# Attention and MLP in one kernel: the same instructions in another planned order, from a new table of key shifts

## The chip, the cores and the metric

The kernel runs on one core of one Trainium2 chip. The metric is the time of one execution on the device, in microseconds. All executions do the same work on the same inputs.

## What is computed

Attention with random features, followed by a two-layer MLP, in float32 on both sides.

```python
batch, n_heads, seq, head_dim = (8, 8, 576, 64)     # q, k, v; omega is 128 x 64
def phi(x):                                         # x is q or k, scaled by 64 ** -0.25
    proj = np.einsum('bhsd,md->bhsm', x, omega)
    h = proj - np.sum(x * x, axis=-1, keepdims=True) / 2.0
    return np.exp(h - np.max(h, axis=-1, keepdims=True)) / np.sqrt(m)
kv = np.einsum('bhsm,bhsd->bhmd', k_p, v)
z = np.sum(k_p, axis=2)
num = np.einsum('bhsm,bhmd->bhsd', q_p, kv)
den = np.einsum('bhsm,bhm->bhs', q_p, z)[..., None] + 1e-06
attn_out = num / den
...
h = x @ w_in                                        # x: 4608 tokens x 512; w_in 512 x 2048
g = h * (1.0 / (1.0 + np.exp(-h)))
return g @ w_out                                    # w_out 2048 x 512
```

## The kernel before

**Attention.** The 64 pairs of batch and head are worked in 32 windows of two heads each. A window projects k and q by omega on TensorE (L372 and L377 for the first eight windows, which fold the squares into the matmul; L372 for the others, with the middle rows apart at L386, L387 or L392). VectorE (DVE) takes the row maxima (L403, L405, L408) and makes biases of them (L411, L412), ScalarE (ACT) takes the exponentials (L433; for a few windows DVE adds the bias at L450 and L443 first and ACT does the whole at L454), GpSimd (POOL) sums the features of k (L462 to L475), and TensorE forms the z sums (L484), the product of features and v (L492), and a transpose of that (L500) through copies on ACT (L497, L505). DVE works out the denominators (L516, L522), POOL divides (L527), TensorE transposes the result (L533), ACT copies it (L537), and TensorE makes the numerator (L554). ACT casts or copies that into xq (L576), and for the first three batches DVE makes the low part (L580).

**MLP.** Every float32 product is done as three float32r products of a high and a low part (L725). Weights come in as 64-bit words that DVE turns into float32 (L607 on ACT, L619, L621 and L625 on DVE) and that ACT and POOL split (L635, L639). Token block 0 is multiplied directly: first layer into the PSUM pool h, ACT's silu (L736, L737), DVE's low part (L741, the unit g_low), second layer into the pool acc. The other eight blocks go in four pairs by a seven-product Strassen scheme, whose operands ACT and DVE split (L767, L771, L783, L787), and whose sums DVE forms (L763, L779, L817, L844). The MLP has 3120 matmuls in all, 576 into ps_h (the first layer of blocks 0 to 2) and 2544 into ps_acc; attention's small matmuls are put between them.

**What sets the order.** The whole program is a list of 3731 units, each with an engine, an assumed duration, what it must come after, the ring buffers and PSUM banks that it takes and frees, and a key: the time at which it is due. Plan.run fills the five engines' lists: of the units that could start at about the soonest moment on an engine it takes the one with the smallest key. Each engine then runs its list strictly in order, and the semaphores make sure of the dependencies. Before planning, keys are shifted by a table, STIR. Each of its 33 entries has a seed, a size and a range of keys; a unit whose key (under 900) lies in the range has its key moved by size times a number from -1 to 1, a hash of the seed and the unit's name. So the table draws one of very many nearby orders; the units, their instructions and their dependencies are the same in each. PSUM has eight banks in three pools, acc 4, h 2 and att 2; before the MLP starts and between its stages attention may take banks of the others, whichever comes free first, so the name of the pool (ps_acc, ps_h, ps_att) can differ for the same unit.

The lines that set this:

```python
            key = u["key"]
            if key < 900.0:
                for seed, size, lo, hi in STIR:
                    if lo <= key < hi:
                        u["key"] += size * (zlib.crc32((str(seed) + repr(n)).encode()) / 2**31 - 1)
...
                p = min((p for p in pick if p[3] <= least + 0.25), key=lambda p: p[2:])
```

## Time and profile before

| what | value |
|---|---|
| median of three runs | 994.75 us (993.66 to 995.33) |
| the profiled execution | 993.29 us |
| its span, first to last instruction | 991.2 us |
| granted clock, mean | 0.998 |
| ACT's table loads between exp and silu | 72 |

The profile is of one execution. A row of a group has the busy time, the mean of one instruction in ns, and the idle time of the engine just before such instructions with what ended it. PE is TensorE, PEld its weight loads, which run beside the matmuls. A busy PE is not always PE at its peak: the ends of matmuls are modelled. A releaser is inferred from semaphores, and where several were waited for the last by the profile is named.

The two parts of the work differ: until about 72 us only attention and the preparation of the weights run; from there to about 800 us attention's remaining windows are woven into the MLP; the rest is the MLP alone.

### The profile page before, as it was taken

The page shows a single profiled execution, that of the slowest core. Times are in us where ns is not written, and L with a number is a line of the kernel's source. Part 1 is how long each engine was busy: PE and PEld are TensorE (multiplying, and loading weights), DVE is VectorE, ACT ScalarE, POOL GpSimd, SP SyncE. Part 2 cuts the span into 40 slices and gives each one's busy share as a digit, 9 for nine tenths or more (in the row PEclk, how much of TensorE's full clock was granted, in tenths as well). Part 3 has the DMA queues.
Part 4 walks back from the last instruction along what each step waited for, and adds up shares of the span by engine and source line. Part 5 has one row for each costly group of instructions (what it writes and reads, how often), then busy time and mean ns, then how long its engine had stood idle before and what let it go on. Part 6 is the DMA issues. An engine that isn't in the chain of part 4 may idle for free.

```text
span 991.2 us, 17002 instructions
## 1 busy us (share of the span) xinstructions
PE 962.2 (97%) x5846; PEld 772.7 (78%) x5846; DVE 779.0 (79%) x1611; ACT 645.7 (65%) x1239; POOL 410.5 (41%) x427
## 2 busy tenths in 40 slices
PE   8889999999999999999999999999999999999998
PEld 7667777777778777777887777788788887888886
DVE  3999999589554898986988999797699966269954
ACT  7899776679778776859758856555275544325442
POOL 3775665867975666686331334333012210000000
PEclk9999999999999999999999999999999999999999
DMA  7579897899988788988667666666555566556562
GB/s 282 160 264 312 311 298 241 309 331 316 293 304 295 252 290 275 302 292 287 215 209 238 212 197 220 229 222 203 184 187 176 179 205 235 192 190 213 193 215 103
DMA packets 103734, 238.70 MB, mean 241 GB/s; under 512 B 13664, under 2 KB 44512, under 8 KB 103648
## 3 DMA queue, kind: packets, MB, share of 16 engines
q1 hardware_dynamic: 103504, 237.54, 71.7%
q8 instruction: 47, 0.77, 0.3%
q14 instruction: 39, 0.32, 0.1%
q10 hardware_dynamic: 144, 0.07, 0.0%
HBM read 193.53 MB, written 44.04 MB: 240 GB/s over the span
## 4 chain that ended last, share of the span: by engine, by line
PE 68%; DVE 16%; ACT 10%; issue 2%; DMA 2%; SPq 0%; DVEq 0%; ACTq 0%
PE ps_acc L725 50%; PE ps_h L725 6%; DVE prod L516 3%; PE ps_att L372 2%; DVE ts L771 2%; PE ps_att L492 2%; DVE g L621 2%; PE ps_h L372 2%; DVE g L619 1%; ACT hk L433 1%; PE ps_att L554 1%; DVE g L625 1%; ACT hq L433 1%; PE ps_att L533 1%; DVE g L763 1%
## 5 line engine op out<-in xcount | busy, mean ns | idle before, releaser
L725 PE MATMUL ps_acc<-ts,w 128*128 128x512 f32 x2544 | 612.3, 394 | 2.0 <-DVE ts L771 1.4
L725 PEld LDWEIGHTS ps_acc<-ts,w 128*128 128x128 f32 x2544 | 468.8, 188 | 102.4 <-DVE ts L771 2.5
L767 ACT CAST ts<-g 128x1024 fp32r<-128x1024 f32 x112 | 118.5, 1062 | 96.5 <-PE ps_acc L725 92.3
L771 DVE TENSOR_TENSOR ts<-g,ts 128x1024 fp32r<-128x1024 f32 x112 | 147.4, 1324 | 37.5 <-ACT ts L767 36.8
L527 POOL TENSOR_TENSOR hq<-hq,rd 128x384 f32<-128x384 f32 x84 | 90.6, 1104 | 168.9 <-DVE rd L522 151.6
L725 PE MATMUL ps_h<-xq,w 128*128 128x512 f32 x576 | 149.6, 400 | 2.5 <-ACT g L758 1.8
L725 PEld LDWEIGHTS ps_h<-xq,w 128*128 128x128 f32 x576 | 104.3, 188 | 25.3 <-ACT g L758 2.6
L817 DVE TENSOR_TENSOR g<-ps_acc,g 128x512 f32<-128x512 f32 x144 | 95.3, 685 | 32.3 <-PE ps_acc L725 31.1
L763 DVE TENSOR_TENSOR g<-g,g 128x1024 f32<-128x1024 f32 x64 | 84.4, 1340 | 5.8 <-ACT g L758 5.5
L462 POOL TENSOR_TENSOR t<-hk 128x256 f32<-128x256 f32 x64 | 53.5, 851 | 74.3 <-ACT hk L454 46.6
L516 DVE CUSTOM_DVE_ANT_0 prod<-hq,ps_att 128x128 f32<-128x128 f32 (+1 forms) x170 | 48.6, 286 | 19.2 <-PE ps_att L484 9.5
L475 POOL TENSOR_TENSOR es<-t,es 128x256 fp32r<-128x256 f32 x32 | 28.4, 889 | 68.2 <-ACT es L471 68.1
L639 POOL TENSOR_TENSOR w<-g,w 128x512 fp32r<-128x512 f32 x32 | 46.6, 1471 | 21.1 <-ACT w L635 18.2
L821 ACT ACTIVATE g<-g 128x1024 f32<-128x1024 f32 x36 | 37.5, 1058 | 26.5 <-DVE g L817 26.3
L783 ACT CAST ts<-xq 128x1024 fp32r<-128x1024 f32 x21 | 22.2, 1059 | 45.6 <-PE ps_acc L725 45.4
L467 POOL TENSOR_TENSOR t<-t,hk 64x128 f32<-64x128 f32 x64 | 40.2, 628 | 11.2 <-ACT hk L433 7.2
L353 ACT ACTIVATE nat<-nat 128x576 f32<-128x576 f32 x48 | 32.3, 705 | 14.5 <-DMA nat<-kn 7.9
L787 DVE TENSOR_TENSOR ts<-xq,ts 128x1024 fp32r<-128x1024 f32 x21 | 27.8, 1324 | 16.8 <-ACT ts L783 16.8
L433 ACT ACTIVATE hk<-ps_att,nbk 128x128 f32<-128x128 f32 x115 | 32.8, 404 | 7.0 <-DVE nbm L411 3.9
L433 ACT ACT_TABLE_LOAD x24 | 30.8, 1283 | 9.8 <-DVE nbk L412 7.4
L844 DVE TENSOR_TENSOR c<-ps_acc,c 128x512 f32<-128x512 f32 x48 | 30.7, 682 | 5.6 <-PE ps_acc L725 5.6
L358 DVE TENSOR_REDUCE sq<-nat 128x9 f32<-128x576 f32 x48 | 34.7, 745 | 0.4
(209 smaller groups left out, 1537.1 us busy)
## 6 DMA issues: line engine op xcount, KB each, us to landing
w<-w_d SPq DMA_DIRECT2D x168, 512.0 KB, 4.2
w<-ws_d SPq DMA_DIRECT2D x48, 512.0 KB, 3.3
rawk<-kT SPq DMA_DIRECT2D x32, 352.0 KB, 4.3
rawq<-qT SPq DMA_DIRECT2D x32, 352.0 KB, 3.9
v<-v SPq DMA_DIRECT2D x32, 320.0 KB, 4.5
out<-c SPq DMA_DIRECT2D x17, 512.0 KB, 4.5
g<-w_in SPq DMA_DIRECT2D x16, 512.0 KB, 5.3
g<-w_out SPq DMA_DIRECT2D x16, 512.0 KB, 4.4
```

The costliest lines, as they stand in the source:

```text
L372: nc.tensor.matmul(ps[:, cols], raw[r, o : o + P], w[r], start=True, stop=n not in FOLD)
L433: nc.scalar.activation(h[:, c], ps[:, i * M : (i + 1) * M], AF.Exp, bias=bias_of(n, who, c), scale=-1.0 if n in FOLD else 1.0)
L462: nc.gpsimd.tensor_tensor(t[:, i], e[:, 5 * i : 5 * i + 2], e[:, 5 * i + 2 : 5 * i + 4], ALU.add)
L467: nc.gpsimd.tensor_tensor(t[r, i - 3, 0], t[r, i - 3, 0], e[r, MID], ALU.add)
L516: nc.vector.tensor_tensor_reduce(out=prod[r], in0=e[r, c], in1=z[r, j * M : (j + 1) * M], scale=1.0, scalar=GUARD, op0=ALU.mult, op1=ALU.a ...
L527: nc.gpsimd.tensor_tensor(e[:, c], e[:, c], rd[:, c].unsqueeze(2).broadcast_to([P, 3, M]), ALU.mult)
L639: nc.gpsimd.tensor_tensor(lo, T["w", i], hi.bitcast(F32), ALU.subtract)
L725: nc.tensor.matmul(ps, w(a), x[:, b], start=first and n == 0, stop=last and n == 2, **more)
L763: nc.vector.tensor_tensor(out, a, b, ALU.subtract)
L767: nc.scalar.copy(g[:, 0], T["g", p, SOURCE[j], u])
L771: nc.vector.tensor_tensor(g[:, 1], T["g", p, SOURCE[j], u], g[:, 0].bitcast(F32), ALU.subtract)
L817: nc.vector.tensor_tensor(to, T["q", p, chain, i], T["g", p, r, i // 2][:, i % 2], ALU.add)
```

## The change

STIR has a new table of 107 entries, each with a fifth number, a mask. A unit's key is moved by an entry only where the hash has none of the mask's bits: with mask 0 all units of the range are moved, with 1 half of them, with 31 one in 32. 31 entries have mask 0, 12 have 1, 17 have 3, 16 have 7, 12 have 15 and 19 have 31. Sizes go from 0.18 to 10.75 (before, from 0.75 to 4.0). Two entries have empty ranges. The old entry that moved every unit under 900 by up to 0.75 is gone; the four entries over the whole span have masks 31, 7, 31 and 15.

```diff
 STIR = (
-    (85063, 0.75, -100, 900), (45882, 1.5, 786, 906), (7545, 0.75, 621, 741), (21412, 1.5, 610, 640),
...
+    (80956, 2.1, -110, 900, 31), (60897, 0.19, -80, 910, 7), (37960, 0.73, -90, 900, 31),
...
 )
...
         for n, u in self.units.items():
             key = u["key"]
-            if key < 900.0:
-                for seed, size, lo, hi in STIR:
-                    if lo <= key < hi:
-                        u["key"] += size * (zlib.crc32((str(seed) + repr(n)).encode()) / 2**31 - 1)
+            for seed, size, lo, hi, mask in STIR:
+                if key < 900.0 and lo <= key < hi:
+                    h = zlib.crc32((str(seed) + repr(n)).encode())
+                    if not h & mask:
+                        u["key"] += size * (h / 2**31 - 1)
```

Every line of the file behind the table stands 20 lower: L725 of before is L745 now, L533 is L553, L580 is L600, and so on. Over the whole list TensorE has 170 stretches of attention between MLP matmuls, where it had 165, and ACT has 74 table loads where it had 72.

**TensorE, end of the lead-in.** Where the MLP's first matmuls (ps_h<-xq,w) stand among the last attention units of windows 3 to 5: transposes of window 3 (ps<-ident,hq), the transpose of window 4's product (ident,kt), the projection of window 5's q (omn,rawq; half,c), the numerator of window 3 (en,kw), window 4's sums (es,ones). Before:

```order
L533 MATMUL ps_att<-ident,hq 128x128 x6
L533 MATMUL ps_h<-ident,hq 128x128 x3
L500 MATMUL ps_acc<-ident,kt 128x128
L372 MATMUL ps_att<-omn,rawq 128x128 x2
L377 MATMUL ps_att<-half,c 128x128 x2
...
L554 MATMUL ps_acc<-en,kw 64x512 x2
L554 MATMUL ps_acc<-en,kw 64x64 x2
L484 MATMUL ps_acc<-es,ones 128x256 x2
L386 MATMUL ps_acc<-omn,rawq 128x128
L387 MATMUL ps_acc<-half,c 128x128
L725 MATMUL ps_h<-xq,w 128x512 x24
```

The same place now:

```order
L553 MATMUL ps_att<-ident,hq 128x128 x6
L553 MATMUL ps_h<-ident,hq 128x128 x3
L406 MATMUL ps_acc<-omn,rawk 128x128
L407 MATMUL ps_acc<-half,c 128x128
L745 MATMUL ps_h<-xq,w 128x512 x3
L574 MATMUL ps_att<-en,kw 64x512 x2
L574 MATMUL ps_att<-en,kw 64x64 x2
L745 MATMUL ps_h<-xq,w 128x512 x6
L520 MATMUL ps_acc<-ident,kt 128x128
L504 MATMUL ps_acc<-es,ones 128x256 x2
L745 MATMUL ps_h<-xq,w 128x512 x15
L392 MATMUL ps_att<-omn,rawq 128x128 x2
```

The first 24 MLP matmuls have moved ahead of window 5's projection of q, nine of them ahead of window 4's transpose, three ahead of window 3's numerator.

**DVE, the same place.** Maxima (L405), a weight's words (L619, L621, L625), sums of squares of windows 8 and 9 (L358), denominators of window 4 (prod,den), the low part of xq of window 3 (the last L580), and the first g_low (ts<-ph). Before:

```order
L580 TENSOR_TENSOR xq<-ps_acc,xq 128x512
L358 TENSOR_REDUCE sq<-nat 128x9 x2
L625 SCALAR_TENSOR_TENSOR g_742<-g_632,g_742 128x512
L405 TENSOR_REDUCE nbq<-ps_att 128x4 x2
...
L516 ISA prod,den<-hq,ps_acc 128x128
L516 ISA den 128x1
L580 TENSOR_TENSOR xq<-ps_acc,xq 128x512
...
L522 RECIPROCAL rd<-den 128x9
L403 TENSOR_REDUCE nbq<-ps_acc 128x1
L619 TENSOR_SCALAR g_742<-g_687 128x512
...
L741 TENSOR_TENSOR ts<-ps_h,ts 128x512
```

The same place now, from the last L580 (L600) on:

```order
L600 TENSOR_TENSOR xq<-ps_att,xq 128x512
L536 ISA prod,den<-hq,ps_acc 128x128
...
L542 RECIPROCAL rd<-den 128x9
L761 TENSOR_TENSOR ts<-ps_h,ts 128x512
L641 SCALAR_TENSOR_TENSOR g_970<-g_970 128x512
L645 SCALAR_TENSOR_TENSOR g_970<-g_852,g_970 128x512
L761 TENSOR_TENSOR ts<-ps_h,ts 128x512
L425 TENSOR_REDUCE nbq<-ps_att 128x4 x2
L423 TENSOR_REDUCE nbq<-ps_acc 128x1
L378 TENSOR_REDUCE sq<-nat 128x9 x2
```

The low part of xq stands ahead of all of window 4's denominators, and the first two g_low stand ahead of window 5's maxima and of the sums of squares.

**TensorE, the middle projection of window 8.** The k projection of window 8 (oms,rawk x8), the matmul of its middle rows (the single oms,rawk and oms,rawq), and window 7's transposes. Before:

```order
L372 MATMUL ps_att<-oms,rawk 128x128 x8
L725 MATMUL ps_h<-xq,w 128x512 x9
L725 MATMUL ps_acc<-ts,w 128x512 x6
L392 MATMUL ps_att<-oms,rawk 128x128
L392 MATMUL ps_att<-oms,rawq 128x128
L533 MATMUL ps_att<-ident,hq 128x128 x3
```

Now:

```order
L392 MATMUL ps_att<-oms,rawk 128x128 x8
L745 MATMUL ps_h<-xq,w 128x512 x3
L745 MATMUL ps_acc<-ts,w 128x512 x9
L745 MATMUL ps_h<-xq,w 128x512 x3
L553 MATMUL ps_att<-ident,hq 128x128 x6
L745 MATMUL ps_h<-xq,w 128x512 x3
L412 MATMUL ps_att<-oms,rawk 128x128
L412 MATMUL ps_att<-oms,rawq 128x128
L553 MATMUL ps_att<-ident,hq 128x128 x3
```

Three more MLP matmuls and the first six of window 7's nine transposes stand ahead of the middle projection.

**DVE, the same place.** From the end of window 7's denominators (rd<-den) to the subtraction that empties window 8's two banks (hk<-ps_att,nbk). Before:

```order
L522 RECIPROCAL rd<-den 128x9
L741 TENSOR_TENSOR ts<-ps_h,ts 128x512
L619 TENSOR_SCALAR g_1964<-g_1872 128x512
L619 TENSOR_SCALAR g_1974<-g_1877 128x512
L621 SCALAR_TENSOR_TENSOR g_1974<-g_1974 128x512
L625 SCALAR_TENSOR_TENSOR g_1974<-g_1877,g_1974 128x512
L621 SCALAR_TENSOR_TENSOR g_1964<-g_1963,g_1964 128x512
L405 TENSOR_REDUCE mxk<-ps_att 128x4 x2
L411 TENSOR_TENSOR nbk<-mxk,sq 128x2x4
L412 SCALAR_TENSOR_TENSOR nbk<-nbk,sq 128x2x4
L450 TENSOR_TENSOR hk<-ps_att,nbk 128x512 x2
```

Now:

```order
L542 RECIPROCAL rd<-den 128x9
L761 TENSOR_TENSOR ts<-ps_h,ts 128x512
L641 SCALAR_TENSOR_TENSOR g_1970<-g_1970 128x512
L645 SCALAR_TENSOR_TENSOR g_1970<-g_1898,g_1970 128x512
L425 TENSOR_REDUCE mxk<-ps_att 128x4 x2
L431 TENSOR_TENSOR nbk<-mxk,sq 128x2x4
L432 SCALAR_TENSOR_TENSOR nbk<-nbk,sq 128x2x4
L470 TENSOR_TENSOR hk<-ps_att,nbk 128x512 x2
```

Two L619 and an L621 that stood between the g_low and the maxima now stand ahead of the denominators.

35 rows, old and new, of the table STIR are left out of this document.

## The prediction

> **What bounds the kernel now.** I read the page first, for the shares and the clock, then the stretches, then TensorE's waits, and last the timeline at the two longest waits. The first lines of the page give the shares over the whole span.
>
> ```profile
> span 991.2 us, 17002 instructions
> PE 962.2 (97%) x5846; PEld 772.7 (78%) x5846; DVE 779.0 (79%) x1611; ACT 645.7 (65%) x1239; POOL 410.5 (41%) x427
> ```
>
> TensorE is busy for 962.2 of 991.2 us, so 29.0 us are idle, and an order that changes no work can win at most those, and part of what is slow inside the busy time. The stretches, cut where the character of the work changes, say where the 29 us lie. The columns are the length, then the busy time of PE, PEld, DVE, ACT and POOL with instruction counts, the granted clock, and DMA.
>
> ```profile
> 25.00:72.00 47.00, 37.54 (x394) 29.40 (x391) 44.19 (x125) 42.43 (x128) 35.77 (x39) 0.96 0.64 209
> 72.00:125.00 53.00, 50.40 (x310) 40.22 (x310) 48.98 (x95) 46.63 (x87) 32.75 (x30) 1.00 0.92 312
> 125.00:250.00 125.00, 120.75 (x790) 95.49 (x787) 102.93 (x266) 97.45 (x174) 85.48 (x90) 1.00 0.89 297
> 250.00:500.00 250.00, 245.17 (x1540) 194.47 (x1539) 185.31 (x424) 184.67 (x404) 166.19 (x166) 1.00 0.83 280
> 500.00:965.00 465.00, 464.56 (x2492) 376.04 (x2490) 376.74 (x663) 250.40 (x395) 82.64 (x87) 1.00 0.63 205
> ```
>
> Idle PE time is 9.46 us from 25 to 72, 2.60 from 72 to 125, 4.25 from 125 to 250, 4.83 from 250 to 500, and 0.44 in the 465 us after that. The second half is bound by TensorE and has nothing left for an order to win. The lead-in is another matter: from 25 to 72 us DVE is busy for 44.19 of 47 us, so it is DVE that bounds it, and only 2.81 us of DVE idle can be squeezed there. What TensorE waited for, longest in total first (columns: us, times, longest):
>
> ```profile
> PE ps_att L372 <- ACT en L537: 2.4, 2, 1.7
> PE ps_att L392 <- DVE hk L450: 1.9, 1, 1.9
> PE ps_h L725 <- ACT g L758: 1.8, 3, 0.8
> PE ps_att L533 <- POOL hq L527: 1.5, 2, 1.1
> PE ps_acc L533 <- POOL hq L527: 1.5, 4, 0.6
> PE ps_acc L725 <- DVE ts L771: 1.4, 3, 0.6
> PE ps_acc L500 <- DMA rawk<-kT: 1.3, 1, 1.3
> PE ps_h L725 <- DVE ts L741: 0.7, 1, 0.7
> ```
>
> No kind of wait is large: the total is many single waits of about 1 us, each at a place of its own. A new order must therefore be judged place by place, and the two largest places are looked at here.
>
> **Term 1, the end of the lead-in.** In the timeline of TensorE at 61 to 71 us (start, length, line, tiles, and in brackets the idle time before it and its releaser):
>
> ```profile
> 61.32 0.55 PE L533 MATMUL ps_h<-ident,hq 128*128 128x128 f32 x3
> 63.13 0.33 PE L500 MATMUL ps_acc<-ident,kt 128*128 128x128 f32 x1 [1.26 <-DMA rawk<-kT]
> 65.13 0.76 PE L372 MATMUL ps_att<-omn,rawq 64*128 64x128 f32 x3 [1.68 <-ACT en L537]
> ...
> 70.92 5.73 PE L725 MATMUL ps_h<-xq,w 128*128 128x512 f32 x24
> ```
>
> Between 61.9 and 65.1 us TensorE does one transpose, and the MLP's first matmul comes at 70.92. The clock answers to that lull, in two stretches just behind it:
>
> ```profile
> 64.00:66.00 2.00, 0.87 (x10) 0.78 (x12) 2.00 (x3) 2.00 (x8) 1.15 (x1) 1.00 0.11 30
> 66.00:68.00 2.00, 2.00 (x25) 2.00 (x23) 2.00 (x4) 2.00 (x8) 0.74 (x2) 0.52 0.11 15
> 68.00:70.00 2.00, 2.00 (x10) 0.95 (x10) 1.73 (x3) 1.88 (x6) 2.00 (x2) 0.63 0.87 299
> ```
>
> The granted clock is 0.52 and 0.63 for 2 us each, which loses 2 x 0.48 + 2 x 0.37 = 1.70 us of TensorE. Together the place costs TensorE 1.26 + 1.68 + 1.70 = 4.64 us. [...]
>
> The new order (first pair of excerpts of the change) puts three of the first 24 L725 matmuls ahead of the numerator of window 3, six more before the L500 transpose that waited, and the other fifteen before the projection that waited; before, all 24 stood behind these. What they need is there earlier: DVE (second pair) writes xq for window 3 (L580) before the denominators of window 4, not in their midst, and the two L405 of window 5 and the two L358 now stand behind the first L741. By their rows those are
>
> ```profile
> 66.22 1.40 DVE L358 TENSOR_REDUCE sq<-nat 128x9 f32<-128x576 f32 x2
> 68.45 1.28 DVE L405 TENSOR_REDUCE nbq<-ps_att 128x4 f32<-128x512 f32 x2
> 71.63 0.69 DVE L580 TENSOR_TENSOR xq<-ps_acc,xq 128x512 fp32r<-128x512 f32 x1
> ```
>
> 1.40 + 1.28 = 2.68 us, taken from in front of the MLP's first g_low (L741) and put behind it; the L580 is 0.69. It is moved, not removed. Ahead of the numerator of window 5 the plan lists 137 units on DVE before and 139 now, the two more, on balance, being one L621 of a weight and one L741, by the means of their groups (the number behind the busy time, in ns)
>
> ```profile
> L621 DVE SCALAR_TENSOR_TENSOR g<-g 128x512 uint32<-128x512 uint32 x16 | 15.6, 975 | 2.4 <-ACT g L607 1.4
> L741 DVE TENSOR_TENSOR ts<-ps_h,ts 128x512 fp32r<-128x512 f32 x16 | 10.9, 682 | 3.4 <-ACT ps_h L737 3.1
> ```
>
> 0.975 + 0.682 = 1.7 us more. So the two bounds are a gain of 2.81 us (DVE's idle gone) and a loss of 1.7 us (DVE as idle as before, and more to do by then). I take a gain of 2.0, near the upper end, because TensorE's own lull and its slow clock lie exactly where matmuls are put.
>
> **Term 2, the middle projection of window 8.** The longest single wait of the span behind the first 10 us is here; TensorE first, then DVE:
>
> ```profile
> 162.26 1.16 PE L372 MATMUL ps_att<-oms,rawk 64*128 64x128 f32 x16
> 163.35 2.34 PE L725 MATMUL ps_h<-xq,w 128*128 128x512 f32 x9
> 165.53 1.52 PE L725 MATMUL ps_acc<-ts,w 128*128 128x512 f32 x6
> 168.92 0.46 PE L392 MATMUL ps_att<-oms,rawk 128*128 128x128 f32 x2 [1.87 <-DVE hk L450]
> 169.52 0.52 PE L533 MATMUL ps_att<-ident,hq 128*128 128x128 f32 x3
> ```
> ```profile
> 161.26 2.07 DVE L619 TENSOR_SCALAR g<-g 128x512 uint32<-128x512 uint32 x2
> 164.70 0.69 DVE L621 SCALAR_TENSOR_TENSOR g<-g,g 128x512 uint32<-128x512 uint32 x1
> 165.30 1.28 DVE L405 TENSOR_REDUCE mxk<-ps_att 128x4 f32<-128x512 f32 x2
> 168.08 1.29 DVE L450 TENSOR_TENSOR hk<-ps_att,nbk 128x512 f32<-128x512 f32 x2
> ```
>
> L392 needs a PSUM bank that L450 empties at about 168.8. Before, 15 L725 matmuls stand between the L372 that fills the banks and L392; now (third pair of excerpts) 18 stand there and six L533 as well. The three more cost 3 x 1.52 / 6 = 0.76 us, the six L533 about 2 x 0.52 = 1.04, together 1.80 us of useful work in the place of a wait of 1.87. On DVE (fourth pair) two L619, two L621 and an L625 stood between the L741 and this L405, 4.04 us from 161.26 to 165.30; now one L621 and one L625 do, so L405 no longer has to come 1.9 us after the L372 that ends at 163.4. Bounds: a gain of 1.87, or nothing if the denominators that now stand ahead of the L741 make DVE late by as much. I take 1.5.
>
> **Term 3, the other waits from 72 to 500 us.** They are 2.60 + 4.25 + 4.83 - 1.87 = 9.81 us, in many places, all of which the new order rearranges. I can't follow each, so I count in the plan's order the handoffs with the least room: transposes (L533) with fewer than six L725 matmuls between their last POOL step and themselves, 13 of windows 4 to 31 before and 10 now, and sums (L484) with as few behind L475, 9 before and 7 now. That is 5 of 22, or 23%, which of 9.81 us is 2.2. But the trace shows only six waits for L527, 3.0 us (rows above), of which none is a microsecond long but one, so what is tight in the list is mostly not late on the chip, and I take half: 1.0. Bounds: a gain of 4.9 (half of them gone), and a loss of 4.9 (half as many again).
>
> **What costs nothing.** The new order has 74 loads of an activation table instead of 72. A load, with its neighbours on ACT:
>
> ```profile
> 170.07 0.48 ACT L537 COPY en<-ps_att 128x384 f32<-128x384 f32 x1 [3.26 <-PE ps_att L533]
> 170.57 1.28 ACT L454 ACT_TABLE_LOAD   x1
> 171.87 1.17 ACT L454 ACTIVATE hk<-hk 128x1152 f32<-128x1152 f32 x1
> ```
>
> It takes 1.28 us and the neighbours stand within 0.02 us of it, so two more are 2.57 us of ACT, which is busy 65% of the span: cover enough, and without the cover 2.57 us on the path. [...] From 500 us on PE has 0.44 us to win, and the list of PE ends in one run of 672 L725 (738 before), and the last four stores stand as they stood: nothing there.
>
> **The sum.** 2.0 + 1.5 + 1.0 = 4.5 us. The profiled execution took 993.29 us (span 991.2 and 2.09 around it), so 988.8 for such an execution. The median of the three runs shown is 994.75, which is 1.46 above it, so the forecast for a median is 990.3 us.
>
> **The rivals.** A measurement of this kernel can tell 0.2%, about 2.0 us, from no change.
>
> *DVE gives nothing back (no change).* The lead-in is DVE's, and DVE's work ahead of window 5 is no less. Then terms 1 and 3 are nothing, and term 2's 1.5 us is all: 993.3. For it speaks 44.19 of 47 us; against it, that DVE is down to 48.98 of 53 and 102.93 of 125 us in the stretches behind, so something other than DVE holds TensorE there too.
>
> *The matmuls pulled forward block the queue (slower).* TensorE runs its list in order. The tenth to twelfth L725 need xq of window 3, which the L554 behind the third feeds through ACT's cast and L580; behind them stand the projections of window 5 (L372, L386), and DVE, ACT and POOL of window 5 behind those. If the L725 wait, window 5 and all after it comes late. The cast costs
>
> ```profile
> 63.97 0.61 ACT L576 CAST xq<-ps_acc 128x512 fp32r<-128x512 f32 x1
> ```
>
> Price: the 1.7 us more that DVE has ahead of window 5, the 2.81 us that DVE then idles once more, and a new wait of cast and L580 (0.61 + 0.69 = 1.30 us): 5.8 us, less term 2's 1.5: 4.3 us more, 999.1. It decides if the wait at those L725 is over about 3 us; below that DVE has other work queued to fill it. For it speaks that only six L725, a transpose and an L484 lie between that L554 and the ones that need it; against, that L580 stands early in DVE's new list.
>
> *Most single waits go (faster by far).* If the order fits the chip as a whole, term 1 gives DVE's 2.81 and the slow clock's 1.70, term 2 all of 1.87, term 3 half of 9.81: 11.3 us, 983.5. Against it: each place has to fit by itself.
>
> **How the numbers follow.** The forecast of a gain of 2 to 7 us has a chance of 0.46, the far gain 0.17, no change 0.15, the blocked queue and its like 0.22. So faster by over 0.2% is 0.63, within 0.2% 0.15, slower 0.22. The terms' own bounds make 994.75 - 2.81 - 1.87 - 4.9 = 985.2 and 994.75 + 1.7 + 4.9 = 1001.4 if all fall one way; the range reaches down to include the far gain and up past the blocked queue's 999.1: 982 to 999.5.
>
> **What would show it.** Right: no dip of the clock between 60 and 75 us, the first L725 (L745 in the new file) at about 68, PE idle from 25 to 72 down by 2 us or more, no wait over 1 us at L392's successor L412, and 500 to 965 unchanged. Wrong: PE idle before 250 us of 16 us again with the waits at other lines, a wait of 3 us or more at the first 24 L745, or idle PE behind 500 us, where there was none.

## The result, and the profile after

The changed kernel takes 1007.81 us (median of 4 runs, 1006.23 to 1010.3), the kernel before beside it on the same chip 994.2 us (992.87 to 995.33). The ratio is 1.0140, 95% interval 1.0115 to 1.0165: slower by 13.6 us, where 4.5 us less had been forecast, and beyond the upper end of the range. The profiled execution took 1010.3 us, its span is 1008.4 us, its mean granted clock 0.989 (0.998 before). One of the six executions of f3_three below, the profiled one, had a clock of 0.751 and took 1197.94 us; its row leaves that execution out, and its profile is not used.

The first lines of the page of the changed kernel:

```profile
span 1008.4 us, 17035 instructions
PE 970.0 (96%) x5846; PEld 777.1 (77%) x5846; DVE 785.4 (78%) x1611; ACT 650.1 (64%) x1241; POOL 408.4 (40%) x427
```

The same matmuls keep TensorE busy 7.8 us longer, and it is idle for 38.4 us instead of 29.0: 9.4 more. The busy part is the clock: 1.1% of 1008.4 us is 11 us at a stopped clock, 0.2% of 991.2 was 2, so 9 us more are lost to it. That holds for these two executions: over all on record the mean clock is 0.990 for the changed kernel and 0.996 for the kernel before, which makes 6 us. The stretches say where (columns as in the prediction):

```profile
25.00:72.00 47.00, 39.58 (x369) 30.72 (x370) 43.11 (x122) 42.68 (x123) 31.52 (x37) 0.93 0.69 228
72.00:125.00 53.00, 49.29 (x321) 39.44 (x321) 47.68 (x92) 43.14 (x90) 30.64 (x28) 1.00 0.86 293
125.00:250.00 125.00, 119.76 (x793) 94.22 (x790) 106.33 (x248) 94.39 (x169) 87.69 (x90) 1.00 0.89 298
250.00:500.00 250.00, 239.97 (x1483) 188.29 (x1482) 177.27 (x406) 186.32 (x398) 160.04 (x159) 0.99 0.82 270
500.00:965.00 465.00, 461.56 (x2487) 374.46 (x2486) 379.87 (x689) 252.63 (x405) 88.61 (x93) 0.99 0.62 203
```

Idle TensorE in them: 7.42, 3.71, 5.24, 10.03 and 3.44 us, before 9.46, 2.60, 4.25, 4.83 and 0.44. The first stretch has the 2 us that the first term promised. All others are worse, and the worst are the two behind 250 us. The waits that are new, or grew (us in total, times, longest):

```profile
PE ps_acc L745 <- DVE c L864: 6.9, 2, 3.8
PE ps_h L553 <- POOL hq L547: 3.2, 4, 1.7
PE ps_att L553 <- ACT hk L453: 3.1, 2, 1.8
PE ps_h L745 <- DVE xq L600: 2.2, 1, 2.2
PE ps_att L553 <- DVE hk L470: 2.1, 1, 2.1
```

The largest did not exist before: MLP matmuls that wait for L864 (L844 before), where DVE adds the last sums of a Strassen pair from the acc banks. TensorE at the first of the two places:

```profile
446.82 1.55 PE L745 MATMUL ps_acc<-ts,w 128*128 128x512 f32 x6
452.19 5.06 PE L745 MATMUL ps_acc<-ts,w 128*128 128x512 f32 x11 [3.82 <-DVE c L864]
```

DVE there (left out are window 20's maxima and biases, between the first two sums, and then the rest of window 18's denominators):

```profile
444.92 0.68 DVE L864 TENSOR_TENSOR c<-ps_acc,c 128x512 f32<-128x512 f32 x1
...
447.44 0.68 DVE L864 TENSOR_TENSOR c<-ps_acc,c 128x512 f32<-128x512 f32 x1
448.05 0.28 DVE L536 CUSTOM_DVE_ANT_0 prod<-hq,ps_h 128x128 f32<-128x128 f32 x1
...
451.38 0.21 DVE L542 RECIPROCAL rd<-den 128x9 f32<-128x9 f32 x1
451.51 1.23 DVE L864 TENSOR_TENSOR c<-ps_acc,c 128x512 f32<-128x512 f32 x2
```

The kernel before, DVE at the same place and at the second one:

```profile
437.21 2.47 DVE L844 TENSOR_TENSOR c<-ps_acc,c 128x512 f32<-128x512 f32 x4
655.70 2.48 DVE L844 TENSOR_TENSOR c<-ps_acc,c 128x512 f32<-128x512 f32 x4
```

Four sums read the same two acc banks: two units a21 and two units b22. Before, they stand together. Now the two a21 come first (444.92 and 447.44, with window 20's maxima and biases between them), then window 18's denominators for 3.5 us, and only then the two b22 (451.51). The next pair's third group of matmuls needs one of these banks and waits for b22. The second place is the same with window 28's maxima and subtractions between a21 (664.24) and b22 (669.67). TensorE there, then DVE, with the rows of window 28 left out:

```profile
665.80 1.53 PE L745 MATMUL ps_acc<-ts,w 128*128 128x512 f32 x6
670.41 2.93 PE L745 MATMUL ps_acc<-ts,w 128*128 128x512 f32 x6 [3.08 <-DVE c L864]
```
```profile
664.24 1.28 DVE L864 TENSOR_TENSOR c<-ps_acc,c 128x512 f32<-128x512 f32 x2
665.44 0.68 DVE L425 TENSOR_REDUCE mxk<-ps_att 128x4 f32<-128x512 f32 x1
...
669.67 1.28 DVE L864 TENSOR_TENSOR c<-ps_acc,c 128x512 f32<-128x512 f32 x2
```

The plan allows this because only a21 is listed as freeing the banks (`free=ch`); b22 reads them too, but is not listed, and in the old order its key, 1 us smaller, kept it near enough. Late in the first wait the clock halves, from 451.0 to 457.8 us (stretches of 2 us of the changed kernel, the clock third from the end):

```profile
450.00:452.00 2.00, 0.00 (x0) 0.00 (x0) 1.79 (x10) 1.07 (x3) 0.85 (x2) 0.75 1.05 335
452.00:454.00 2.00, 1.81 (x4) 1.49 (x5) 1.39 (x3) 0.00 (x0) 1.14 (x2) 0.50 1.04 394
454.00:456.00 2.00, 2.00 (x6) 1.55 (x5) 0.00 (x0) 0.83 (x2) 2.00 (x3) 0.50 0.35 137
456.00:458.00 2.00, 2.00 (x7) 1.61 (x7) 0.00 (x0) 1.33 (x2) 1.92 (x3) 0.54 0.00 0
```

2 x (0.25 + 0.5 + 0.5 + 0.46) = 3.4 us of clock, 0.6 of them in the last 1.2 us of the wait, which ends at 452.19, and 2.8 behind it. The trace's clock records have another such stretch, 6.8 us at half clock, from 669.5 us on; the wait there ends at 670.41, and 2.9 us are behind it. In this one execution the waits and the slow clock at the two places add up to 3.82 + 3.08 + 2.8 + 2.9 = 12.6 us; its span is 17.2 us over that of the kernel before, and the medians are 13.6 us apart. Whether the two places cost so much is what the experiments ask first.

### The profile page after: what moved, and what is told of

The parts are those of the page before. It is cut to its first block, busy times and chain, and to the rows that moved or that the text cites. A ratio compares the mean times of both kernels' runs of the same rounds, so it can differ in the third digit from the quotient of the medians.

```text
span 1008.4 us, 17035 instructions
## 1 busy us (share of the span) xinstructions
PE 970.0 (96%) x5846; PEld 777.1 (77%) x5846; DVE 785.4 (78%) x1611; ACT 650.1 (64%) x1241; POOL 408.4 (40%) x427
## 4 chain that ended last, share of the span: by engine, by line
PE 64%; DVE 21%; ACT 8%; DMA 3%; issue 2%; POOL 1%; SPq 0%; DVEq 0%; ACTq 0%; POOLq 0%
PE ps_acc L745 45%; PE ps_h L745 6%; DVE ts L791 3%; DVE prod L536 3%; PE ps_att L392 2%; DVE g L783 2%; DVE g L639 2%; DVE g L641 2%; PE ps_att L553 1%; ACT hk L453 1%; PE ps_att L512 1%; PE ps_h L392 1%; DMA nat<-qn 1%; DVE g L645 1%; DVE mxk L425 1%
## 5 line engine op out<-in xcount | busy, mean ns | idle before, releaser
L745 PE MATMUL ps_acc<-ts,w 128*128 128x512 f32 x2544 | 617.5, 396 | 8.5 <-DVE c L864 6.9
L745 PEld LDWEIGHTS ps_acc<-ts,w 128*128 128x128 f32 x2544 | 472.0, 189 | 109.9 <-DVE c L864 7.7
L791 DVE TENSOR_TENSOR ts<-g,ts 128x1024 fp32r<-128x1024 f32 x112 | 147.8, 1326 | 34.5 <-ACT ts L787 33.9
L745 PE MATMUL ps_h<-xq,w 128*128 128x512 f32 x576 | 150.4, 401 | 3.0 <-DVE xq L600 2.2
L547 POOL TENSOR_TENSOR hq<-hq,rd 128x384 f32<-128x384 f32 x84 | 94.2, 1147 | 137.9 <-DVE rd L542 130.4
L745 PEld LDWEIGHTS ps_h<-xq,w 128*128 128x128 f32 x576 | 103.9, 188 | 25.7 <-DVE xq L600 2.5
L495 POOL TENSOR_TENSOR es<-t,es 128x256 fp32r<-128x256 f32 x32 | 25.8, 808 | 101.5 <-ACT es L491 95.8
L536 DVE CUSTOM_DVE_ANT_0 prod<-hq,ps_att 128x128 f32<-128x128 f32 (+1 forms) x150 | 42.9, 286 | 19.3 <-PE ps_att L520 8.0
L453 ACT ACTIVATE hk<-ps_att,nbk 128x128 f32<-128x128 f32 x131 | 36.7, 390 | 5.7 <-DVE nbk L432 2.4
L536 DVE CUSTOM_DVE_ANT_0 prod<-hq,ps_h 128x128 f32<-128x128 f32 (+1 forms) x110 | 31.5, 286 | 10.4 <-PE ps_h L504 5.7
L557 ACT COPY en<-ps_att 128x384 f32<-128x384 f32 x63 | 29.8, 503 | 13.4 <-PE ps_att L553 13.3
```

Of the source, the lines that this page charges most:

```text
L453: nc.scalar.activation(h[:, c], ps[:, i * M : (i + 1) * M], AF.Exp, bias=bias_of(n, who, c), scale=-1.0 if n in FOLD else 1.0)
L536: nc.vector.tensor_tensor_reduce(out=prod[r], in0=e[r, c], in1=z[r, j * M : (j + 1) * M], scale=1.0, scalar=GUARD, op0=ALU.mult, op1=ALU.a ...
L547: nc.gpsimd.tensor_tensor(e[:, c], e[:, c], rd[:, c].unsqueeze(2).broadcast_to([P, 3, M]), ALU.mult)
L745: nc.tensor.matmul(ps, w(a), x[:, b], start=first and n == 0, stop=last and n == 2, **more)
L791: nc.vector.tensor_tensor(g[:, 1], T["g", p, SOURCE[j], u], g[:, 0].bitcast(F32), ALU.subtract)
```

## The experiments

The theories: *banks* (the late b22 is the cause, with the clock behind it), *lead-in* (the forecast's own ground, the first 110 us, loses by itself), *spread* (many tight hand-overs; the first expectations say many small waits). All runs in one table; each ratio is to the kernel before on the same chip (993.1 to 994.2 us). Where the text gives a gain or a loss in us, it is the difference of two ratios times 994 us; the intervals of the two together leave some 3 us of it uncertain. Idle is span less TensorE's busy time, of the profiled execution.

| kernel | us | ratio (95%) | PE idle, us | clock |
|---|---|---|---|---|
| before | 994.2 | | 29.0 | 0.998 |
| changed | 1007.8 | 1.0140 (1.0115 to 1.0165) | 38.4 | 0.989 |
| e1_both | 1001.9 | 1.0078 (1.0054 to 1.0102) | 33.9 | 0.995 |
| e2_first | 1006.6 | 1.0122 (1.0095 to 1.0149) | 34.0 | 0.990 |
| e3_second | 1003.8 | 1.0099 (1.0079 to 1.0119) | 35.2 | 0.993 |
| e4_mirror | 1003.8 | 1.0100 (1.0078 to 1.0123) | 36.7 | 0.994 |
| e5_lead | 997.8 | 1.0038 (1.0023 to 1.0053) | 29.0 | 0.995 |
| e6_early | 1004.9 | 1.0112 (1.0097 to 1.0128) | 35.3 | 0.991 |
| e7_plan | 1011.6 | 1.0179 (1.0162 to 1.0196) | 40.9 | 0.986 |
| e8_lead | 1007.5 | 1.0141 (1.0123 to 1.0158) | 36.9 | 0.995 |
| e9_hold | 1004.6 | 1.0111 (1.0077 to 1.0144) | 35.4 | 0.994 |
| d1_draw | 1017.6 | 1.0242 (1.0200 to 1.0283) | 43.7 | 0.988 |
| d2_draw | 1016.2 | 1.0227 (1.0190 to 1.0264) | 39.7 | 0.990 |
| d3_draw | 1021.4 | 1.0280 (1.0208 to 1.0352) | 48.9 | 0.988 |
| f1_first | 1001.0 | 1.0072 (1.0055 to 1.0089) | 34.0 | 0.991 |
| f2_mid | 992.2 | 0.9985 (0.9971 to 0.9999) | 28.5 | 0.995 |
| f3_three | 999.2 | 1.0058 (1.0039 to 1.0077) | | |
| f4_turns | 999.6 | 1.0052 (1.0033 to 1.0072) | 30.7 | 0.996 |
| g1_fills | 991.8 | 0.9987 (0.9977 to 0.9997) | 25.3 | 0.995 |

Most kernels take the finished plan and move a few units in it just before the instructions are issued; each line of the list takes units out and puts them ahead of another (side 0) or behind it (side 1):

```diff
-        for u in plan.run():
+        order = plan.run()
+        for names, where, side in (
+            ((("b22", 0, 0), ("b22", 0, 1)), ("a21", 0, 0), 0),
+            ((("b22", 1, 0), ("b22", 1, 1)), ("a21", 1, 0), 0),
+        ):
+            moved = [plan.units[n] for n in names]
+            order = [u for u in order if u["name"] not in names]
+            at = [u["name"] for u in order].index(where) + side
+            order[at:at] = moved
+        for u in order:
```

**The late sums.** These two lines are e1_both, on the changed kernel. e2_first has the first of them alone, e3_second the second.

> The changed kernel, with one edit: the DVE sums b22 of pairs 0 and 1 (L864, which read the two PSUM banks of chain d) are moved up to stand right ahead of the first a21 of their pair; every other engine's list is unchanged. Bank theory (the slowdown is that these sums stand behind a window's denominators or maxima, TensorE waits 3.8 and 3.1 us for the banks, and its clock is halved for 6.8 us behind each wait): both waits of L745 for L864 gone, no half clock near 451 and 669 us, 6.9 us of waits and about 5.8 us of slow clock won, so about 995 (993 to 998). Lead-in theory (the MLP matmuls pulled forward block TensorE's queue and all comes late from 100 us on): nothing won there, 1005 to 1009. Many-small-waits theory (each of some forty waits a little): at most the 6.9 us, about 1001.

> The same edit for pair 0 alone (the place at 448 us). Bank theory: 3.8 us of wait and about 2.8 us of slow clock won, about 1001 (999 to 1003), and the wait and the half clock at 669 us still there. Lead-in theory: 1005 to 1009.

> The same edit for pair 1 alone (the place at 667 us). Bank theory: 3.1 us of wait and about 3.0 us of slow clock won, about 1001.5 (999 to 1004), and the wait and the half clock at 448 us still there. Lead-in theory: 1005 to 1009.

The wait for L864 is gone in e1_both, and so are the half clocks at 451 and 669 us (the clock is 1.00 from 448 to 454 and from 640 to 700 us). Its three largest waits, those of the first 10 us aside:

```profile
PE ps_att L553 <- ACT hk L453: 3.7, 3, 2.1
PE ps_h L553 <- POOL hq L547: 2.5, 4, 1.4
PE ps_h L745 <- DVE xq L600: 2.2, 1, 2.2
```

But of 1.40% only 0.62% came back, 6.2 us, and 7.8 us stay lost: 1001.9 us is what the many-small-waits theory expected at most, not the 995 of the bank theory. Moving one pair alone gave 1.8 and 4.1 us. The 1.8 is within the noise, and e2_first, at 1006.6, missed the 999 to 1003 us that the bank theory expected of it. A part of what the profile showed at the two places was handed on, as at the first of them in e1_both:

```profile
450.99 1.66 PE L745 MATMUL ps_acc<-ts,w 128*128 128x512 f32 x6 [1.61 <-ACT g L830]
```

The starts of the MLP matmuls tell the two places apart, since TensorE's list is the same in both kernels: in the profiled executions the changed kernel is 0.4 us behind e1_both at the 1080th, ahead of the first place, 4.2 at the 1440th, behind it, and 8.3 from the 1900th to the end. So the two places are a cause, not the whole.

e4_mirror does the reverse, on the kernel before: b22 of pairs 0 and 1 is moved behind the units that stand between in the changed kernel.

```diff
+            ((("b22", 0, 1), ("b22", 0, 0)), ("deep", 1, 0, 2), 0),
+            ((("top", 20, "k", 1), ("top", 20, "k", 0), ("nb", 20, "k"), ("ssum", 21, "k"), ("ssum", 21, "q")), ("b22", 0, 1), 0),
+            ((("b22", 1, 1), ("b22", 1, 0)), ("deep", 2, 0, 2), 0),
+            ((("low", 28, "q", 0), ("low", 28, "q", 1), ("xd", 2, 0)), ("b22", 1, 1), 0),
```

> The kernel before, with the fault put in: b22 of pair 0 (L844) stands behind the denominators of window 18, the maxima and bias of window 20 and two sums of squares, b22 of pair 1 behind the lowering of window 28 and one subtraction; each is issued just ahead of the matmul that takes its bank. TensorE's list is unchanged. Bank theory: waits of about 3.7 and 3.1 us of L725 for L844, each followed by a half clock, so 5 to 13 us slower than before, 999 to 1007. Lead-in theory and many-small-waits theory: at most the waits themselves where nothing hides them, 994 to 1001, without a half clock.

(In it a quarter of the output of pairs 0 and 1 is stored before its last sum is added.) It loses 1.00%, 9.9 us, and its wait has the same name as in the changed kernel:

```profile
PE ps_acc L725 <- DVE c L844: 8.0, 2, 5.1
```

Its MLP matmuls are 0.8 us ahead of those of the kernel before at the 1080th, 5.4 us behind at the 1440th and 10.5 behind from the 1900th on. That a bank's late readers cost this much while TensorE's list is untouched is shown. What the other 7.8 us are is the next question.

**Parts of the two tables.** e5_lead is e1_both with the old table for keys under 110 us; e6_early has the new table under 250 us and the old one behind, e8_lead the same with 72 us. OLD is the old table with mask 0.

```diff
-            for seed, size, lo, hi, mask in STIR:
+            for seed, size, lo, hi, mask in (OLD if key < 110 else STIR):
```

> The changed kernel with the old table for units whose key is under 110 us and the new one for the rest, and with the sums b22 of pairs 0 and 1 moved ahead of a21 as in e1_both. Against e1_both (1001.9 us) it differs by the lead-in and the first 40 us of the MLP alone. If the 8 us that e1_both still lost were lost there (lead-in theory), it takes about 995 us (993 to 998), and the lag behind the kernel before is under 1.5 us at the 360th MLP matmul. If they are lost in many tight hand-overs from 110 to 500 us (spread theory), it stays at 1000 to 1003 us, the lag growing after that matmul. No wait for a sum at 451 or 669 us by either.

> The changed kernel with the new table for units whose key is under 250 us and the old one for the rest; the four last sums of each pair then stand together again without any move. If the late sums are the whole cause (bank theory alone), it takes the time of the kernel before, 993 to 995.5 us. If the first 250 us of the new order lose by themselves what e1_both still lacked at its 360th to 1080th MLP matmul (3.5 to 7 us), it takes 998 to 1001 us.

> The changed kernel with the new table for units whose key is under 72 us alone, the old one for the rest; the last sums of each pair stand together. The lead-in theory (the new lead-in loses 3 to 5 us by pulling matmuls ahead of windows 3 to 5) expects 997 to 999 us. The spread theory expects 993 to 996 us. My forecast's first term, taken by itself, expects 2 us less than before, 992 us.

e5_lead wins 4.0 us over e1_both (0.40%, uncertain by 0.28), half of what was open; at 997.8 us it is at the upper end of what the lead-in theory expected. The lag of its MLP matmuls behind the kernel before is 1.1 us at the 360th and 1.0 at the 420th, against 4.8 at both in e1_both. (Where the two orders place a group of attention's matmuls differently, as from the 361st on, the lag jumps by 2.4 us for a few matmuls.) It is idle no longer than the kernel before. So the new order of the first 110 us does cost some 4 us. But e6_early and e8_lead, which have no late sum, lose 11 and 14 us, more than any theory gave. Both have waits that neither parent has. First e6_early, then e8_lead; their lines stand 13 lower than the changed kernel's, L566 is L553 there:

```profile
431.25 0.55 PE L566 MATMUL ps_h<-ident,hq 128*128 128x128 f32 x3 [3.11 <-POOL hq L560]
...
441.55 0.52 PE L566 MATMUL ps_h<-ident,hq 128*128 128x128 f32 x3 [2.62 <-issue]
```
```profile
149.69 0.91 PE L566 MATMUL ps_att<-ident,hq 128*128 128x128 f32 x6 [3.38 <-ACT hk L466]
```

A part of a table has no price of its own: where it is joined to another, the plan behind it is a new one, with accidents of its own. e6_early and e8_lead therefore tell nothing of the lead-in, and e5_lead's 4.0 us only as much as a new join can.

**The plan told of the bank.** e7_plan lists b22 as freeing the banks too:

```diff
-                add(("b22", p, m), "DVE", 0.6, key, lambda m=m: c_add(p, "22", "22", "d", m), after=[me, ("a22", p, m)])
+                add(("b22", p, m), "DVE", 0.6, key, lambda m=m: c_add(p, "22", "22", "d", m), after=[me, ("a22", p, m)], free=ch)
```

> The changed kernel with one word more in the plan: b22 too counts as a reader that frees the banks of P7's chain, so that the plan puts the next level's third group of matmuls behind b22. The bank theory expects the waits of 3.8 and 3.1 us for a sum and the half clocks behind them to go, as in e1_both: 1002 us (999 to 1004), since the order ahead of 430 us is nearly the same. If the waits were a symptom of DVE being late in that stretch, other work of TensorE waits there in their place, the half clocks stay, and it takes 1005 to 1010 us.

The wait for L864 goes, and others come at the same two stretches, at 453 and 672 us, with slow matmuls behind them: six L745 take 2.76 us at 454.27 and 1.65 at 457.30, three L553 0.88 us at 672.57 and 0.49 at 668.37. It is slower than the changed kernel:

```profile
PE ps_h L553 <- DVE nbk L431: 3.7, 1, 3.7
PE ps_att L553 <- ACT hk L453: 3.6, 3, 1.8
PE ps_h L504 <- ACT es L491: 3.3, 1, 3.3
```

The bank theory expected 999 to 1004 us, so its remedy by the plan fails. On DVE b22 stands where it stood, behind the denominators and the maxima; the plan only put other work of TensorE ahead, and that work waits for units of DVE and ACT that are late there, as the second theory of this run had it (for 1005 to 1010 us). What e1_both won, it won by moving four units and nothing else.

**Other draws.** d1_draw and d2_draw are the kernel before with 1 and 2 added to every seed, d3_draw the changed kernel with 1 added.

```diff
-                        u["key"] += size * (zlib.crc32((str(seed) + repr(n)).encode()) / 2**31 - 1)
+                        u["key"] += size * (zlib.crc32((str(seed + 1) + repr(n)).encode()) / 2**31 - 1)
```

> The kernel before with 1 added to each seed of its table: another draw of the same sizes and ranges. Its plan has b22 behind a21 with a window's maxima between, for pair 0 and for pair 1. If orders of such a table lie evenly around the kernel before, as my prediction took it, and only late sums cost, it takes 1000 to 1004 us (as e4_mirror). If the kernel before is a rare order and a fresh one meets many tight hand-overs (pick theory), 1005 to 1015 us, with several waits of TensorE of over 2 us elsewhere.

> The kernel before with 2 added to each seed. No sum is late in its plan. Even orders: 990 to 997 us. Pick theory: 998 to 1008 us, idle time of TensorE of 36 us or more against 29.

> The changed kernel with 1 added to each seed. Its plan has b22 late for pair 1 alone. Even orders with the late sum: 996 to 1001 us. Pick theory: 1002 to 1014 us.

All three lose 2.27 to 2.80%, 23 to 28 us, more than the pick theory gave. d2_draw has no late sum at all. Its stretches:

```profile
25.00:72.00 47.00, 40.19 (x387) 32.04 (x388) 41.69 (x112) 40.47 (x115) 30.95 (x35) 0.89 0.72 230
72.00:125.00 53.00, 47.18 (x263) 37.16 (x263) 46.28 (x93) 41.11 (x80) 30.73 (x29) 0.94 0.73 241
125.00:250.00 125.00, 117.03 (x761) 92.32 (x757) 99.21 (x240) 92.61 (x162) 75.79 (x80) 0.99 0.84 285
```

6.81, 5.82 and 7.97 us of idle TensorE up to 250 us, 20.6 against 16.3 before, and a clock of 0.89 and 0.94. These three orders, of the same kind with other seeds, are thus 2 to 3% slower than the one at hand (by two executions each; those of d3_draw are 1% apart). The changed kernel, with 1.4%, is better than each of them. The old order is no middle of such orders; how rare it is, three draws can't say.

**The first term as one move.** f1_first is the kernel before with its own table, and on TensorE nine of the first 24 MLP matmuls ahead of window 4's transpose and nine ahead of window 5's projection, without what the new order moves on DVE; e9_hold is the reverse in e1_both, window 5's projection put back ahead of the fifteen.

```diff
+            ((("s1", 0, 0, 0), ("s1", 0, 0, 1), ("s1", 0, 0, 2)), ("ktt", 4), 0),
+            ((("s1", 0, 8, 0), ("s1", 0, 8, 1), ("s1", 0, 8, 2)), ("proj", 5, "q"), 0),
```
```diff
+            ((("proj", 5, "q"), ("mid", 5, "q")), ("s1", 0, 0, 3), 0),
```

> The kernel before with its own table, and on TensorE alone nine of the first 24 MLP matmuls moved ahead of window 4's transpose of the kt product and nine ahead of window 5's projection of q: the first term of my prediction as a single move. My forecast expects 2 us less than before (991.5 to 992.5 us of 993.7), no dip of the clock at 66 us and no wait of 1.3 and 1.7 us at 62 to 65 us. The blocked-queue theory expects a wait at those matmuls, window 5 late, and 1 to 5 us more than before.

> e1_both with one thing more: window 5's projection of q and of its middle rows moved on TensorE ahead of the fifteen MLP matmuls that had been pulled in front of it (they wait 2.2 us for the low part of xq). If the 4 us that the new lead-in loses (e1_both 1001.9 against e5_lead 997.8 us) come from this blocked queue, it takes 997 to 999 us, and the lag behind the kernel before is 1 to 2 us at the 420th MLP matmul (4.7 in e1_both). If the lead-in loses in many places, it stays at 1000 to 1003 us with a lag of 4 us or more there.

f1_first loses 7 us instead of winning 2. TensorE in it:

```profile
60.11 0.55 PE L533 MATMUL ps_h<-ident,hq 128*128 128x128 f32 x3
64.68 4.21 PE L725 MATMUL ps_h<-xq,w 128*128 128x512 f32 x9 [4.03 <-ACT en L537]
...
83.99 4.57 PE L725 MATMUL ps_h<-xq,w 128*128 128x512 f32 x12 [3.59 <-DVE ts L741]
```

ACT, which ends that wait:

```profile
64.07 0.56 ACT L537 COPY en<-ps_h 128x384 f32<-128x384 f32 x1
```

The nine matmuls have their xq, but their bank of ps_h holds window 3's last transposes until ACT has copied them out at 64.63. Window 5 comes late behind that, and TensorE waits again at 84 us. The rival that matmuls pulled forward block the queue is thus real, in the kernel before. In the changed kernel the first three MLP matmuls wait for no bank, and there the rival decides nothing: e9_hold, which undoes it there, is not faster than e1_both (1004.6 against 1001.9), and lags by 7.4 us at the 420th matmul where 1 to 2 were expected.

**Waits filled one by one.** f2_mid, on the kernel before, is the second term alone: nine MLP matmuls ahead of window 8's middle projection. f3_three has the moves of f1_first and f2_mid, and two units ahead of window 6's transpose. f4_turns fills three waits of e1_both, at the transposes of windows 5, 6 and 7, with nine, three and twelve matmuls. g1_fills is f2_mid and two fills more. In this order:

```diff
+            ((("s2", 13, 2), ("s2", 13, 3), ("s1", 0, 7, 0)), ("mids", 8), 0),
...
+            ((("s1", 0, 12, 0), ("s1", 0, 12, 1)), ("ktt", 6), 0),
...
+            ((("s1", 0, 3, 3), ("s2", 2, 0), ("s2", 2, 1)), ("turn", 5, 1), 0),
+            ((("s1", 0, 5, 3),), ("turn", 6, 1), 0),
+            ((("s1", 0, 14, 3), ("s2", 13, 3), ("s1", 0, 7, 0), ("s1", 0, 7, 1)), ("turn", 7, 0), 0),
...
+            ((("s1", 0, 5, 3),), ("turn", 6, 1), 0),
+            ((("pr", 0, 4, 5),), ("z", 16), 0),
```

> The kernel before with its own table, and on TensorE alone nine more MLP matmuls (2.2 us) pulled ahead of window 8's middle projection, which waits 1.87 us: the second term as a single move. My forecast expects 1.5 us less, 992.2 us. If the wait is only handed on (to the transposes or to the matmuls of the next group, as in the changed kernel, where it stands at a transpose with 2.15 us), nothing: 993.7 us, within 0.2%.

> Both moves together in the kernel before, and six MLP matmuls (1.5 us) pulled ahead of window 6's transpose of the kt product, which waits 1.15 us. If waits filled with matmuls add up: 993.7 less 2.0, 1.5 and 1.1, so 989 us. If each is handed on: 993 to 995 us, with as much idle time of TensorE as before (29 us).

> e1_both, and on TensorE alone nine, three and eighteen... in all 24 MLP matmuls pulled ahead of the transposes of windows 5, 6 and 7, which wait 1.8 to 2.1, 1.3 and 2.2 us for ACT and DVE. If the new order's loss from 107 to 175 us lies in where TensorE has these transposes, 4 us of e1_both's 1001.9 come back: 998 us (997 to 999.5), and the lag at the 420th MLP matmul falls from 4.7 to about 1 us. If ACT and DVE are late there whatever TensorE does, the waits come again behind: 1000.5 to 1003.5 us.

> f2_mid, and in the same way three MLP matmuls (0.75 us) pulled ahead of window 6's last two transposes, which wait 0.68 us for POOL, and six (1.5 us) ahead of window 16's sums, which wait 1.27 us for ACT; all these matmuls accumulate in banks that they already hold, or take one that is long free. If a wait can be filled wherever the matmul put there needs no bank that the waiting work holds: 1.5 + 0.7 + 1.3 less than before, 990.5 us (989 to 992.5). If waits are handed on: 992 to 994.5 us.

f2_mid wins 0.15% (0.01 to 0.29%), 1.5 us, as the second term said; the interval reaches from 0.1 to 2.9 us. The wait of 1.87 us is gone from L392; the transposes behind wait for 0.66 and 0.27 us:

```profile
171.28 0.52 PE L533 MATMUL ps_att<-ident,hq 128*128 128x128 f32 x3 [0.66 <-ACT en L537]
172.07 0.52 PE L533 MATMUL ps_att<-ident,hq 128*128 128x128 f32 x3 [0.27 <-DVE hq L443]
```

So half of the wait was handed on. In the profiled execution the MLP matmuls ahead of the place start 0.5 us later than in the kernel before, those behind it 0.2 us earlier: 0.7 us are won there, and as much in g1_fills, which has the same fill.

f3_three is f1_first and f2_mid added up (0.72 less 0.15%, measured 0.58%): the third fill shows nothing. f4_turns wins 2.6 us of the 4 it was meant to, which is within the noise of the two ratios; its lag at the 420th matmul is 3.1 us where about 1 was expected, so a part of these waits was handed on. g1_fills is faster than both kernels, by 0.13% (0.03 to 0.23%) of the kernel before; its idle time is 25.3 us instead of 29.0, but its two further fills can't be told from f2_mid by time.

## Why the prediction was wrong

**The step that failed most** is the last sentence on what costs nothing: "From 500 us on PE has 0.44 us to win ... nothing there". That a stretch has nothing to win says nothing of what it can lose. Idle TensorE from 500 to 965 us went from 0.44 to 3.44 us, 3.08 of it one wait, and the clock was halved for 6.8 us from 669.5 us on. The same fault stands at 450 us. The slack that was counted for term 3 was of data alone (transposes behind POOL, sums behind POOL); the banks that a reader on DVE still holds were not counted. Undone by four moved units, the two places give back 6.2 us of 13.9, the one behind 500 us alone 4.1 (e3_second); made in the old order, the two cost 9.9.

**The signs.** Those named for being right came true about the first two terms' places: 2.04 us less idle time from 25 to 72 us, no half clock between 60 and 75 (the clock there is 1.00; in e1_both, whose list there is the same, fourteen L745 from 69.58 us on take 5.06 us instead of 3.47, and the clock from 72 to 90 us is 0.93), no wait at L412 of window 8. The time was lost elsewhere, and two of the signs of being wrong show it: idle TensorE from 25 to 250 us is 16.4 us against 16.3, with the waits at other lines, and there is idle time behind 500 us.

**Term 1** (2.0 us won) came out in its own stretch: idle TensorE from 25 to 72 us is 2.04 us less. It was given back behind: 1.11 us more from 72 to 125, 0.99 more from 125 to 250, and the clock of the stretch itself fell from 0.96 to 0.93. The changed kernel there:

```profile
62.25 0.95 PE L745 MATMUL ps_h<-xq,w 128*128 128x512 f32 x3
...
70.36 3.47 PE L745 MATMUL ps_h<-xq,w 128*128 128x512 f32 x14 [2.23 <-DVE xq L600]
73.75 0.49 PE L392 MATMUL ps_att<-omn,rawq 64*128 64x128 f32 x4
```

The MLP starts 8.7 us earlier (70.92 before), and window 5's projection of q 8.6 us later (65.13 before): an exchange, no gain. Windows 5 and 6 then wait at their transposes (the 3.1 us for L453 above). The step that failed is "What they need is there earlier". The low part of window 3's xq is only 2.0 us earlier (69.62 us, 71.63 before), since DVE had 2.37 us of a weight's words in front of it (two L639, from 67.33 on); the matmuls that need it were moved ahead by more, and waited. Moved in the kernel before, on TensorE alone, they lack the bank, and it costs 7 us (f1_first). Of the order of the first 110 us as a whole, e5_lead puts the cost at 4.0 us; f4_turns puts 2.6 us of it, within the noise, at three transposes. Which instructions of DVE, ACT or POOL make those late was not found.

**Term 2** (1.5 us) did not come in the changed kernel, where its lower bound came true: "nothing if the denominators ... make DVE late by as much". DVE, then TensorE, in the changed kernel:

```profile
165.08 0.22 DVE L542 RECIPROCAL rd<-den 128x9 f32<-128x9 f32 x1
...
167.91 1.28 DVE L425 TENSOR_REDUCE mxk<-ps_att 128x4 f32<-128x512 f32 x2
...
171.29 1.29 DVE L470 TENSOR_TENSOR hk<-ps_att,nbk 128x512 f32<-128x512 f32 x2
```
```profile
172.13 1.12 PE L553 MATMUL ps_att<-ident,hq 128*128 128x128 f32 x6 [2.15 <-DVE hk L470]
```

The denominators end at 165.30, where L405 had begun before; the maxima start at 167.91 instead of 165.30, and L470 empties the banks from 171.29 on. The wait, 2.15 instead of 1.87 us, only changed its name, from L392 to the transpose that was pulled ahead of it. As a single move (f2_mid) the term's 1.5 us agree with the measured time, but by the traces 0.7 us are won at the place: the agreement to the tenth is luck.

**Term 3** (1.0 us won, bounds 4.9 each way): from 72 to 500 us idle TensorE rose by 1.11 + 0.99 + 5.20 = 7.3 us, 3.82 of it the late sum. With that sum it is beyond the bound of 4.9, without it, at 3.5, inside. The bounds were laid evenly about the kernel before. The three draws stand 23 to 28 us behind it, so it is no middle of its neighbours, and a new order must be expected to lose unless each hand-over is followed.

**The rivals.** "Matmuls pulled forward block the queue" had waits of 0.53 and 2.23 us at its place, under the 3 us from which it was to decide, and e9_hold shows that in the changed kernel it does not decide. It gave the right sign for a reason that the runs don't bear out, and its 999.1 us, like the 1001.4 to which the terms' own bounds reached, lies well under the measured 1007.8. The 74 table loads were not tried apart; no new wait names one.

**What stays open.** e5_lead, without late sums and with the old lead-in, is still 0.38% behind, 3.8 us. Its idle time is that of the kernel before. In its profiled execution TensorE is busy for 965.7 us instead of 962.2, and its clock is 0.93 from 25 to 72 us and 0.97 from 125 to 190, where the kernel before has 0.96 and 1.00: 0.03 x 47 + 0.03 x 65 = some 3.4 us of TensorE. That would be all of it, but a lower clock is not worth its full loss: of 54 executions of the kernel before, the 30 with a mean clock of 0.997 or 0.998 have a mean span of 991.4 us, the 12 with 0.992 or 0.993 one of 992.6, 1.2 us for some 5 us at a stopped clock. So this rest has no cause shown.

## What to carry to other kernels

When a matmul is moved ahead, or a reader moved back, ask of its PSUM bank as of its data: who reads the bank last, on which engine, and what stands before that reader in its list. A time measured for one of many possible orders is not the middle of the others; here a fresh draw cost 23 to 28 us, and parts of the two orders joined cost 4 to 14. What did win was one wait filled by matmuls that need no bank of the work that waits, and it won a part of the wait: 0.15% by time, 0.7 of 1.87 us by the traces.

## What the runs showed of the hardware

The half clock is not in proportion to the wait. In the changed kernel the waits of 3.82 and 3.08 us each came with 6.8 us at half clock, from 451.0 and 669.5 us on. In e4_mirror a wait of 5.05 us came with half as much:

```profile
446.00:448.00 2.00, 0.72 (x2) 0.63 (x3) 1.47 (x3) 0.00 (x0) 0.12 (x1) 0.79 1.02 357
448.00:450.00 2.00, 2.00 (x6) 1.41 (x5) 0.96 (x1) 0.00 (x0) 2.00 (x1) 0.50 0.77 301
450.00:452.00 2.00, 2.00 (x12) 1.82 (x11) 0.00 (x0) 1.75 (x5) 1.92 (x3) 0.86 0.01 2
```

That is 2 x (0.21 + 0.5 + 0.14) = 1.7 us lost. Nor does the same order bring the same clock: up to 430 us the changed kernel and e1_both have one and the same. Behind the wait for L600 (2.23 us in the changed kernel, 2.22 in e1_both) the clock from 72 to 90 us is 1.00 in the changed kernel and 0.93 in e1_both; behind a wait for L453 (1.79 and 2.14 us) it is 1.00 and 0.50 from 112 to 114 us. In the traces of the two kernels the stretches at half clock are 3.4 us long (from 66.1 us before, from 34.6 and 55.1 us in the changed kernel) or 6.8 (the two above), but for those that the end of the span cuts off. The mean clock of the 54 executions of the kernel before goes from 0.992 to 0.998, a difference of some 6 us at a stopped clock. One profiled execution therefore says what a wait may cost in clock only to within one such stretch of 3.4 us or two, each 1.7 us of TensorE, and the share of the clock in the lost time is better read from the mean clock of several executions.
